# Tile 0 transposed before its scale is known: a linear-attention and MLP kernel with its start reordered

## The chip, the cores and the metric

The kernel runs on one core of one Trainium2 chip. The metric is the device time of one execution, in microseconds (us); lower is better. A core has TensorE (PE in the profile; PEld is its loading of weights), VectorE (DVE), ScalarE (ACT), GpSimd (POOL) and SyncE (SP). SP here only issues DMAs. Each engine works through its own instructions in order.

## The reference

`x` has 2048 tokens of 512 features. The block normalises each token, and adds to `x` the output of a linear attention with 32 heads and that of an MLP with a squared ReLU, both reading the same normalised tokens. All is in float32.

```python
x = A_x
xn = _layernorm(x)                      # (x - mean) / sqrt(var + 1e-5)
# attention: 32 heads of 16
q, k, v = split(xn @ wqkv)
phi = lambda t: where(t > 0, t + 1, exp(t)) + 1e-6
kv  = einsum("bhsd,bhse->bhde", phi(k), v);   z = sum over s of phi(k)
num = einsum("bhqd,bhde->bhqe", phi(q), kv);  den = phi(q) . z + 1e-6
att = (num / den) @ wo
# MLP, F = 1376
h   = relu(xn @ w1 + b1) ** 2
mlp = h @ w2 + b2
out = x + att + mlp
```

## The kernel before, in words

The 2048 tokens are 16 tiles of 128 tokens; four tiles make a block of 512. A float32 operand is split into a high part (rounded to the type fp32r) and a low part (what is left), and a product is three matmuls: high by high, high by low and low by high. "Chunk j" is one of the four groups of 128 features. Order on every engine is the order in which the program was recorded (`manual_schedule`).

**First phase, tiles 0 to 15 (L594 to L903).** For each tile i: statistics on VectorE (`measure`), 1/deviation as a power on GpSimd (`roots`), the normalised tile `xp[i]`, its transposed columns, and the split of the columns into `xsb` (`high` on ScalarE, `low` on VectorE). `project` multiplies the columns with the key weights `wk` (split into `wkh` by `heads_k` on ScalarE and `wkl` by `rests_k`) into a PSUM bank `pk`. `phi_k` makes phi of the keys, `parts` splits it, `tokens` splits the token-major `xp[i]` into `tok[i]`, and `kx(i)` accumulates, over all tiles, the product of tokens and keys. The last feature of `xp[i]` is overwritten with ones first (`ones(i)`, on GpSimd), so that the same product also holds the sum of the keys; the values are worked out from the accumulated product later. Weights and tokens are loaded on SP's queue.

**How tiles are transposed.** Tiles 0 to 2 (`i < NDVE`, which is 3) go through TensorE, against an identity, 128 by 128 at a time (`turned_pe`). The others go through DRAM: the normalised tile is written to `via`, read back in four moves that put blocks of 32 rows where they belong (`regroup`, `move`), and VectorE's transposition of 32 by 32 blocks ends it (`turn`). Such a tile is written into `xp` in a grouped order (`gjc`), and `tokens` and `ones` look at `i >= NDVE` to know it. `ones(i)` of such a tile has to come after `via` was written, since it overwrites a feature.

The columns of tiles 0 to 7 are kept in DRAM (`xTd`) for the second half of the kernel, which reads them back around 197 us (`keep_t` writes them; for tiles 0 to 2 ScalarE first copies them out of PSUM).

**The start, L525 to L669.** `WARM` matmuls of zeros run first. Tiles 0 and 1 and the four chunks of the key weights `rk` are loaded on SP's queue; ScalarE's queue holds one small load named `touch`, ahead of its table load. Tiles 0 to 2 share the three `pk` banks, and the products of tile 0 and tile 1 are interleaved by hand, chunk by chunk (`some`, `rest`). `load_x(4, x4)` fetches tiles 4 to 7, one megabyte, in one DMA; a one-column copy on GpSimd from `xp[1]` into `x4` just ahead of it makes the load wait until tile 1 is normalised.

**Later phases** (L905 on): the MLP and queries of two blocks at a time in a seven-product scheme, the attention's output and the sums. The change doesn't touch them.

## Time and profile before

| what | value |
|---|---|
| time, median of 3 runs | 408.75 us (408.64 to 409.38) |
| profiled execution, its own time | 409.03 us |
| its span | 407.3 us |
| PE busy | 402.2 us of the span |
| DVE, ACT, POOL busy | 308.0, 268.4, 49.7 us |
| granted TensorE clock in the windows shown | 1.00 |
| first transpose on TensorE | at 6.14 us |
| kx(0) | from 16.35 us |

How to read the lines of the profile. A timeline row is: start in us from the span's start, how long the merged instructions took, engine, line of the kernel, operation, output<-inputs by the program's names, shapes, how many; in brackets the idle time of that engine before it and what ended it. `SPq` is SP's DMA queue; its rows give the time of the issue, not of the transfer. A row of the DMA view ends with the size and the median us from issue to landing. A row of the stretches ("0.00:8.00 8.00, ...") gives the length, then busy time and count of PE, PEld, DVE, ACT and POOL, the granted clock, the busy share of the DMA engines and GB/s. A row of the chain is start, length, engine and line. A row of one line's instructions gives shortest/median/longest duration in ns.

### The profile page before, as it was taken

The numbers are of one execution on the slowest core, as the hardware profiler recorded it, in microseconds if no ns is written. First come the engines' busy times: TensorE is split into PE (matmuls) and PEld (weight loads), VectorE is DVE, ScalarE is ACT, GpSimd is POOL, SyncE is SP. The second block draws the span as 40 slices with busy tenths as digits, with TensorE's granted clock in tenths as the row PEclk, the third lists the DMA queues.
The fourth block names the chain that finished last, engine by engine and source line by source line (L and its number), as shares of the span: only waits on it lengthen the run. The fifth ranks groups of instructions, "written<-read, shape, count | busy, mean of one in ns | idle before, by whom it ended". The sixth has DMA issues, their size and how long they took to land.

```text
span 407.3 us, 5632 instructions
## 1 busy us (share of the span) xinstructions
PE 402.2 (99%) x1939; PEld 331.0 (81%) x1939; DVE 308.0 (76%) x559; ACT 268.4 (66%) x466; POOL 49.7 (12%) x81
## 2 busy tenths in 40 slices
PE   8999999999999999999999999999999999999996
PEld 7888888888788888888878888888888888878885
DVE  5886666587898989988349997667989676449833
ACT  5677677556887788886818752667687856828520
POOL 5444333220000000030000300000000200001200
PEclk9999999999999999999999999999999999999999
DMA  6857646900432231380564903311222880034612
GB/s 212 278 175 224 208 163 192 256 27 0 120 90 80 77 103 27 121 200 16 217 228 146 194 19 113 106 53 52 52 80 50 226 189 26 0 108 151 105 26 103
DMA packets 46830, 49.00 MB, mean 120 GB/s; under 512 B 8337, under 2 KB 31121, under 8 KB 46546
## 3 DMA queue, kind: packets, MB, share of 16 engines
q1 hardware_dynamic: 44418, 44.46, 35.4%
q0 software_dynamic: 2304, 4.20, 6.5%
q8 instruction: 15, 0.25, 0.2%
q14 instruction: 13, 0.11, 0.1%
q10 hardware_dynamic: 80, 0.00, 0.0%
HBM read 37.76 MB, written 9.70 MB: 117 GB/s over the span
## 4 chain that ended last, share of the span: by engine, by line
PE 98%; DMA 1%; DVE 1%; ACT 0%; issue 0%
PE acc L133 37%; PE b L497 33%; PE pk L378 11%; PE kx L398 11%; PE acc L508 2%; PE pz L133 1%; DMA x<-in_A_x_dram 1%; PE b L133 1%; PE pz0b L133 1%; PE acc L515 0%; PE pt L310 0%; DVE st L236 0%; PE pkv L937 0%; PE pm L954 0%; PE end L133 0%; PE end L508 0%
## 5 line engine op out<-in xcount | busy, mean ns | idle before, releaser
L133 PE MATMUL acc<-w2r,s 128*128 128x512 f32 x477 | 112.8, 390 | 0.0
L133 PEld LDWEIGHTS acc<-w2r,s 128*128 128x128 f32 x477 | 89.4, 188 | 19.3 <-issue 0.7
L497 PE MATMUL b<-T,aop 128*128 128x512 f32 x336 | 83.5, 389 | 0.0
L497 PEld LDWEIGHTS b<-T,aop 128*128 128x128 f32 x336 | 63.0, 188 | 13.9 <-ACT t L114 0.8
L1075 POOL DMA_DIRECT2D res<-in_B_b_dram x16 | 14.4, 1067 | 276.7 <-DVE pt L438 90.4
L398 PE MATMUL kx<-pk,tok 128*128 128x512 f32 x192 | 46.0, 389 | 0.0
L398 PEld LDWEIGHTS kx<-pk,tok 128*128 128x128 f32 x192 | 36.0, 188 | 7.6 <-ACT pk L114 0.2
L497 PE MATMUL b<-xs0h,aop 128*128 128x512 f32 x112 | 36.9, 390 | 0.0
L133 PE MATMUL acc<-mh,aTsr 128*128 128x512 f32 x112 | 35.6, 389 | 0.0
L1083 DVE TENSOR_TENSOR res<-acc,res 128x512 f32<-128x512 f32 x16 | 10.7, 689 | 20.5 <-PE acc L133 19.2
L114 ACT ACTIVATE aop<-S 128x512 fp32r<-128x512 f32 x28 | 17.5, 624 | 12.5 <-DVE S L735 12.5
L359 POOL TENSOR_TENSOR tok<-xp,tok 128x512 fp32r<-128x512 f32 x15 | 20.2, 1344 | 39.6 <-ACT tok L114 39.6
L497 PEld LDWEIGHTS b<-xs0h,aop 128*128 128x128 f32 x112 | 21.0, 188 | 4.4
L133 PEld LDWEIGHTS acc<-mh,aTsr 128*128 128x128 f32 x112 | 21.0, 188 | 4.4
L125 DVE TENSOR_TENSOR w2r<-r,w2r 128x512 fp32r<-128x512 f32 (+2 forms) x35 | 23.8, 682 | 0.5 <-ACT w2r L114 0.4
L122 DVE TENSOR_TENSOR aop<-S,aop 128x512 fp32r<-128x512 f32 x28 | 19.3, 688 | 4.8 <-ACT aop L114 4.4
L122 DVE TENSOR_TENSOR s<-c,s 128x512 fp32r<-128x512 f32 x20 | 13.6, 689 | 11.4 <-ACT s L114 11.3
L497 PE MATMUL b<-xs0l,aop 128*128 128x512 f32 x56 | 21.8, 389 | 0.0
L133 PE MATMUL acc<-ml,aTsr 128*128 128x512 f32 x56 | 21.8, 389 | 0.0
L114 ACT ACTIVATE w2r<-r 128x512 fp32r<-128x512 f32 x32 | 19.6, 619 | 3.3 <-DMA out_dram<-res 2.0
L497 PE MATMUL b<-xs1h,aop 128*128 128x512 f32 x56 | 19.5, 389 | 0.0
L114 ACT ACTIVATE T<-Tf 128x512 fp32r<-128x512 f32 x16 | 9.5, 624 | 14.4 <-DVE Tf L678 14.3
(195 smaller groups left out, 751.6 us busy)
## 6 DMA issues: line engine op xcount, KB each, us to landing
r<-in_B_w_dram SPq DMA_DIRECT2D x49, 256.0 KB, 3.2
res<-in_A_x_dram SPq DMA_DIRECT2D x8, 512.0 KB, 4.2
res<-in_B_b_dram POOLq DMA_DIRECT2D x16, 256.0 KB, 5.7
out_dram<-res SPq DMA_DIRECT2D x15, 256.0 KB, 2.1
via<-xp SPq DMA_DIRECT2D x5, 512.0 KB, 2.6
xg<-via SPq DMA_DIRECT2D x20, 128.0 KB, 2.8
xTd<-t SPq DMA_DIRECT2D x8, 256.0 KB, 3.4
x<-in_A_x_dram SPq DMA_DIRECT2D x4, 512.0 KB, 4.1
```

Source lines behind the costliest of these rows:

```text
L114: nc.scalar.activation(o, i, AF.Copy, bias=bias)
L122: ENG[el].tensor_tensor(out=l, in0=src, in1=f32(h), op=OP.subtract)
L125: nc.vector.tensor_tensor(out=l, in0=src, in1=f32(h), op=OP.subtract)
L133: nc.tensor.matmul(ps, lhsT=a[u], rhs=b[v], start=first and n == 0, stop=last and n == 2)
L359: ENG[el].tensor_tensor(out=l, in0=src, in1=f32(h), op=OP.subtract)
L378: nc.tensor.matmul(ps, lhsT=cols(i)[u][:, j, slot(i)], rhs=w[v][:, j, :], start=first and n == 0, stop=last and n == len(steps) - 1)
L398: nc.tensor.matmul(kxp[c], lhsT=tok[i][:, u, c * P:(c + 1) * P], rhs=pk[i][:, v], start=i == 0 and (u, v) == first, stop=i == NT - 1 and ( ...
L497: nc.tensor.matmul(ps, lhsT=a[u][:, j * P:(j + 1) * P], rhs=b[v][:, j, :], start=first and j == 0 and n == 0, stop=last and j == 1 and n == 2,
L508: nc.tensor.matmul(ps, lhsT=s[u][:, k * P:(k + 1) * P], rhs=w2s[NF - 1][u][:, a:z], start=first and u == 0, stop=stop and u == 1)
L1075: nc.gpsimd.dma_start(r[:, i], b2[None, :].partition_broadcast(P), accum_op=OP.add)
L1083: nc.vector.tensor_tensor(out=r[:, a:z], in0=ps, in1=r[:, a:z], op=OP.add)
```

## The change

Tile 0 is centred as soon as its mean is known and transposed like that; 1/deviation is a factor of each token, so it is put in where the tokens stand on partitions. The keys of tile 0 come out of the projection unscaled, and phi of them is worked out with the scale (`scale0`, and its negative `less0`, which GpSimd makes). The normalised tile, still needed for `tok[0]`, is made later by a ScalarE activation with that scale, written in the grouped order into the place of the raw tile `x0`, so tile 0 joins the set `grouped`. Its normalised columns, which `keep0` used to store from PSUM, come through `via0`: written after `keep1`, read back by four moves at tile 9, turned by VectorE and stored at tile 10. Tile 0 is loaded in two halves of 256 features on SP's queue, tile 1 on ScalarE's queue; `touch` is gone; `WARM` is 9 instead of 11. Tiles 0 and 1 share one `group`, so one power serves both. The hand-written order of the first products changes, and `rests_k("dve", 1)` comes earlier.

The diff, cut where a line only moves:

```diff
-    WARM = 11
+    WARM = 9
...
-    touch = keep.tile([D // Q * 4, 1], F32, name="touch")
-    nc.scalar.dma_start(touch, wqkv.rearrange("(a b) c -> a b c", b=Q // 4)[:, 0, D:D + 1])
     nc.scalar.preload_act_table_set("natural_log_exp_and_others")
...
+    grouped = {*range(NDVE, NT)}
...
-    def load_x(i, t):
+    def load_x(i, t, eng=nc.sync):
...
@@ turned_pe
-        ones(i)
+        if i:
+            ones(i)
...
@@ ones
-        nc.gpsimd.memset(xp[i][:, D - 1:] if i < NDVE else xp[i][:, NJ - 1, P - 1:], 1.0)
+        nc.gpsimd.memset(xp[i][:, NJ - 1, P - 1:] if i in grouped else xp[i][:, D - 1:], 1.0)
...
@@ the loads
-    for i in range(2):
-        load_x(i, t[:, i:i + 1])
+    xr[0] = t[:, 0]
+    left, right = slice(0, D // 2), slice(D // 2, D)
+    for a in (left, right):
+        nc.sync.dma_start(xr[0][:, a], xf[:P, a])
+    load_x(1, t[:, 1:], nc.scalar)
...
@@ the start
-    two_tiles = group(0), group(1)
-    for t in two_tiles:
-        measure(t)
-        roots(*t)
-    for k in range(2):
-        a = slice(k * D // 2, (k + 1) * D // 2)
-        nc.vector.tensor_scalar(xp[0][:, a], xr[0][:, a], two_tiles[0][2][:, 0, 0:1], two_tiles[0][3][:, 0, :1],
-                                op0=OP.subtract, op1=OP.mult)
-    high, low, keep0 = transposed(0, 2)
+    two_tiles = group(0, 1)
+    _, st, mv, y = two_tiles
+    for k, a in enumerate((left, right)):
+        nc.vector.bn_stats(st[:, k, :], xr[0][:, a])
+    nc.vector.bn_aggr(mv[:, 0, :], st[:, :2, :])
+    for a in (left, right):
+        nc.vector.tensor_scalar(xp[0][:, a], xr[0][:, a], mv[:, 0, 0:1], None, op0=OP.subtract)
+    high, low, _ = transposed(0, 2)
+    high()
+    high(1)
     heads_k(0)
-    high()
+    measure(two_tiles, 1)
+    roots(*two_tiles)
+    low()
+    some(0, 0, (0,), True)
+    some(0, 1, (0,))
     rests_k("pool", 0)
-    some(0, 0, (0,), True)
-    normalise(*two_tiles[1])
+    nc.vector.tensor_scalar(xp[1], xr[1], mv[:, 1, 0:1], y[:, 0, 1:2], op0=OP.subtract, op1=OP.mult)
+    low(1)
+    heads_k(1)
+    some(0, 0, (1,))
+    some(0, 1, (1,))
     high1, low1, keep1 = transposed(1, 2)
-    heads_k(1)
+    scale0 = y[:, 0, 0:1]
+    less0 = y[:, 1, 0:1]
+    nc.gpsimd.tensor_scalar(less0, scale0, -1.0, None, op0=OP.mult)
     nc.gpsimd.tensor_copy(x4[:, 0, :1], xp[1][:, :1])
     load_x(4, x4)
...
@@ after the products of tiles 0 and 1
-    keep0()
     keep1()
+    xp0 = xr[0].rearrange("p (g n) -> p g n", g=NJ)
+    nc.scalar.activation(xp0.rearrange("p g (j c) -> p g j c", j=NJ), gjc(xp[0]), AF.Copy, scale=scale0)
+    xp[0] = xp0
+    grouped.add(0)
+    via0 = dram.tile([P, NJ, P], F32, name="via0")
+    nc.sync.dma_start(via0, xp0)
+    ones(0)
...
-    phi_k(0, pks[0])
+    kp[0] = w512("k0", "p", 6)
+    kept = w512("k0r", "p", 6)
+    nc.scalar.activation(kp[0], pks[0], AF.Relu, scale=less0)
+    nc.vector.tensor_scalar(kept, pks[0], scale0, 0.0, op0=OP.mult, op1=OP.max)
+    nc.scalar.activation(kp[0], kp[0], AF.Exp, scale=-1.0)
+    nc.vector.tensor_tensor(out=kp[0], in0=kept, in1=kp[0], op=OP.add)
...
@@ tile 9
             load_o()
+            xg0 = w512("xg0", "raw", 6).rearrange("p (g n) -> p g n", g=NJ)
+            of_0 = via0.rearrange("(r t) g n -> g t r n", r=NJ)
+            for g in range(NJ):
+                nc.sync.dma_start(xg0[32 * g:32 * (g + 1)], of_0[g])
...
@@ tile 10
+            t0 = w512("t0", "p", 6).rearrange("p (j t) -> p j t", j=NJ)
+            turn(t0, xg0)
+            nc.sync.dma_start(xTd[0][:, :, slot(0)], t0)
```

Three places in the order of the instructions, before and then after. The semaphores in brackets are what an instruction waits for; DMAHW3 and the like are those of DMAs.

VectorE from its first instruction, before: `st0`, `mv0`, `y0` are tile 0's statistics, mean and variance, and root; `st1` and so on tile 1's; `x0` holds both raw tiles.

```order
L236 BN_STATS st0_143<-x0_112 128x6 [waits DMAHW1_49]
L237 BN_AGGR mv0_144<-st0_143 128x2 [waits DVE_49]
L247 TENSOR_SCALAR y0_145<-mv0_144 128x1 [waits DVE_49]
L236 BN_STATS st1_146<-x0_112 128x6 [waits DMAHW2_49]
L237 BN_AGGR mv1_147<-st1_146 128x2 [waits DVE_49]
L247 TENSOR_SCALAR y1_148<-mv1_147 128x1 [waits DVE_49]
L600 TENSOR_SCALAR xp0_80<-x0_112,mv0_144,y0_145 128x256 [waits Pool_49]
L600 TENSOR_SCALAR xp0_80<-x0_112,mv0_144,y0_145 128x256
L270 TENSOR_SCALAR xp0_80<-x0_112,mv1_147,y1_148 128x512 [waits Pool_49]
```

VectorE after, from its first instruction:

```order
L600 BN_STATS st0_140<-x0_108 128x6 [waits DMAHW0_49]
L600 BN_STATS st0_140<-x0_108 128x6 [waits DMAHW1_49]
L601 BN_AGGR mv0_141<-st0_140 128x2 [waits DVE_49]
L603 TENSOR_SCALAR xp0_78<-x0_108,mv0_141 128x256 [waits DVE_49]
L603 TENSOR_SCALAR xp0_78<-x0_108,mv0_141 128x256
L235 BN_STATS st0_140<-x0_108 128x6 [waits DMAHW3_49]
L236 BN_AGGR mv0_141<-st0_140 128x2 [waits DVE_49]
L246 TENSOR_SCALAR y0_142<-mv0_141 128x2 [waits DVE_49]
L329 TENSOR_TENSOR xs1l_75<-pt00_148,xs1h_74 128x2x128 [waits Activation_49]
L614 TENSOR_SCALAR xp0_78<-x0_108,mv0_141,y0_142 128x512 [waits Pool_49]
```

Tile 0's subtraction no longer waits for GpSimd, and tile 1's statistics stand behind it.

GpSimd from the first power to the low part of tile 0's tokens, before (`y2` and `y3` belong to tiles 2 and 3; the L348 rows are the memsets of ones, of tiles 0, 1 and 2 in this order):

```order
L248 TENSOR_TENSOR y0_145<-y0_145,power_99 128x1 [waits DVE_49,Pool_49]
L248 TENSOR_TENSOR y1_148<-y1_148,power_99 128x1 [waits DVE_49]
L348 MEMSET xp0_80 128x1 [waits DVE_49,PE_49]
L583 TENSOR_TENSOR wkl_73<-rk_113,wkh_72 128x512 [waits DMAHW3_49,Activation_49]
L348 MEMSET xp0_80 128x1 [waits DVE_49,PE_49]
L611 COPY x4_134<-xp0_80 128x1
L247 TENSOR_SCALAR y2_197<-mv2_196 128x1 [waits DVE_49]
L248 TENSOR_TENSOR y2_197<-y2_197,power_99 128x1 [waits Pool_49]
L247 TENSOR_SCALAR y3_209<-mv3_208 128x1 [waits DVE_49]
L248 TENSOR_TENSOR y3_209<-y3_209,power_99 128x1 [waits Pool_49]
L348 MEMSET xp0_80 128x1 [waits DVE_49,PE_49]
L359 TENSOR_TENSOR tok0_279<-xp0_80,tok0_279 128x512 [waits Activation_49]
```

GpSimd after, over the same stretch (the L348 rows are now those of tiles 1, 0 and 2):

```order
L247 TENSOR_TENSOR y0_142<-y0_142,power_97 128x2 [waits DVE_49,Pool_49]
L586 TENSOR_TENSOR wkl_71<-rk_109,wkh_70 128x512 [waits DMAHW2_49,Activation_49]
L348 MEMSET xp0_78 128x1 [waits DVE_49,PE_49]
L622 TENSOR_SCALAR y0_142<-y0_142 128x1 [waits Pool_49]
L624 COPY x4_131<-xp0_78 128x1
L246 TENSOR_SCALAR y2_191<-mv2_190 128x1 [waits DVE_49]
L247 TENSOR_TENSOR y2_191<-y2_191,power_97 128x1 [waits Pool_49]
L246 TENSOR_SCALAR y3_202<-mv3_201 128x1 [waits DVE_49]
L247 TENSOR_TENSOR y3_202<-y3_202,power_97 128x1 [waits Pool_49]
L348 MEMSET x0_108 128x1 [waits DMAHW3_49,DMAHW1_49,Activation_49]
L348 MEMSET xp0_78 128x1 [waits DVE_49,PE_49]
L359 TENSOR_TENSOR tok0_274<-x0_108,tok0_274 128x4x4x32 [waits DMAHW0_49,Activation_49]
```

Tile 0's memset moved from the third place to the tenth and waits for DMAs, the one on DMAHW3 being the write of `via0`. The negation L622 stands ahead of the pacing copy L624.

SP's queue from the load of tiles 4 to 7, before:

```order
L161 DMA x4_134<-in_A_x_dram 128x4x512 [waits DMAHW1_49,Pool_49]
L338 DMA xTd0_93<-t0_226 512x1x128 [waits DMAHW2_49,Activation_49]
L338 DMA xTd0_93<-t1_230 512x1x128 [waits DMAHW3_49,Activation_49]
L283 DMA via3_236<-xp0_80 128x512 [waits DMAHW4_49,DVE_49]
L161 DMA x8_135<-in_A_x_dram 128x2x512 [waits DMAHW5_49]
```

SP's queue after, from the same load:

```order
L160 DMA x4_131<-in_A_x_dram 128x4x512 [waits DMAHW1_49,Pool_49]
L338 DMA xTd0_91<-t1_219 512x1x128 [waits DMAHW2_49,Activation_49]
L658 DMA via0_224<-x0_108 128x512 [waits DMAHW3_49,Activation_49]
L282 DMA via3_229<-xp0_78 128x512 [waits DMAHW4_49,DVE_49]
L160 DMA x8_132<-in_A_x_dram 128x2x512 [waits DMAHW5_49]
```

Tile 0's transposed store gave its place to the write of `via0`, which is third behind the megabyte. On ScalarE the copy of tile 0's tokens stands ahead of that of its keys in both kernels.

More of the change, by code (lines that the diff above doesn't have):

```diff
@@ L627 @@
     heads_k(2)
-    rests_k("dve", 1)
     high1(1)
```

13 lines of the change are left out of this document (5 added, 8 removed).

## Prediction

> **What bounds the kernel now.** I read the page's engine shares first, then the chain that ended last. All times are microseconds from the span's start unless they are called durations.
>
> ```profile
> PE 402.2 (99%) x1939; PEld 331.0 (81%) x1939; DVE 308.0 (76%) x559; ACT 268.4 (66%) x466; POOL 49.7 (12%) x81
> PE 98%; DMA 1%; DVE 1%; ACT 0%; issue 0%
> 0.00:8.00 8.00, 6.28 (x32) 5.69 (x33) 3.70 (x11) 3.28 (x6) 4.46 (x17) 1.00 0.75 256
> 8.00:16.00 8.00, 8.00 (x38) 6.30 (x38) 7.17 (x15) 5.50 (x13) 3.66 (x9) 1.00 0.83 246
> 24.00:407.00 383.00, 379.92 (x1837) 312.48 (x1835) 289.79 (x520) 253.76 (x438) 38.44 (x51) 1.00 0.40 114
> ```
>
> TensorE is the chain, and from 8.0 it hardly rests. The change removes no product. It can move the end in two ways only: by starting the unbroken stream of products sooner, or by tearing a hole into it. The chain in order of time shows where the stream begins and where the accumulation kx, the first reader of tile 0's keys and tokens, starts:
>
> ```profile
> 0.79 2.85 DMA x<-in_A_x_dram
> 7.99 4.38 PE pk L378 x19
> 16.51 5.47 PE kx L398 x24
> ```
>
> **The start.** Timeline rows of the load, VectorE, TensorE and ScalarE, and the landings of the loads from the DMA view (issue, then duration to landing):
>
> ```profile
> 1.25 0.41 SPq L161 DMA_DIRECT2D x<-in_A_x_dram  x1
> x<-in_A_x_dram SPq DMA_DIRECT2D x1, 256.0 KB, 3.1
> rk<-in_A_wqkv_dram SPq DMA_DIRECT2D x1, 256.0 KB, 4.3
> 3.66 0.69 DVE L236 BATCH_NORM_STATS2 st<-x 128x6 f32<-128x512 f32 x1 [3.66 <-DMA x<-in_A_x_dram]
> 4.39 0.18 DVE L237 BATCH_NORM_AGGREGATE mv<-st 128x2 f32<-128x6 f32 x1
> 5.68 0.73 DVE L600 TENSOR_SCALAR xp<-x,mv,y 128x256 f32<-128x256 f32 x2
> 6.54 0.55 DVE L270 TENSOR_SCALAR xp<-x,mv,y 128x512 f32<-128x512 f32 x1
> 6.14 0.76 PE L310 MATMUL pt<-ident,xp 128*128 128x128 f32 x4 [0.74 <-DVE xp L600]
> 8.53 0.39 PE L378 MATMUL pk<-wkl,xs1h 128*128 128x512 f32 x1
> 6.62 0.39 ACT L326 ACTIVATE xs1h<-pt 128x256 fp32r<-128x256 f32 x1 [0.75 <-PE pt L310]
> 6.90 0.62 ACT L114 ACTIVATE wkh<-rk 128x512 fp32r<-128x512 f32 x1
> ```
>
> Removed in front of the first transpose: GpSimd's power and tile 1's statistics, which today lie between the load's landing at 3.65 and L600 at 5.68. Added: a second statistics instruction. Neither a 256-wide statistics instruction nor a load of half a tile is in the trace. I take 0.42 for the first, since the 256-wide subtraction takes 0.41 (two of them span 0.73, stepped by 0.32) and the 512-wide statistics 0.69; at 0.69 it would cost 0.27 more. The right half lands at about 3.65, when the whole tile lands now, if tile 1's load on ScalarE's queue stays out of its way. It lands at 1.25 + 3.1 = 4.35, as tile 1 does now, if those 256 KB go ahead of it. So the first centred half is ready at 3.65 + 0.42 + 0.05 + 0.18 + 0.05 + 0.41 = 4.75, or at 5.45. The first transposes start at 4.8 to 5.5 instead of 6.14, a gain of 0.65 to 1.35.
>
> The Trainium skill (DMA: Bandwidth & Descriptors, "Queues, rings and completion order") says that a DMA engine alternates between the queues that have work, a packet at a time. By it tile 1 is served between the two halves, and the sum below would end at its upper figure; with the two loads in order of issue it would end at its lower one. No row of before has two large loads on two queues.
>
> That gain doesn't survive to the third product. ScalarE copies both halves of tile 0 and then the weights. The first copy starts 0.48 after the transposes (6.62 − 6.14), so at 5.3 to 6.0; two copies and wkh of chunk 0 (0.39 and 0.62, overlapping by about 0.1) end at 6.5 to 7.2. The weights of chunk 1 landed at 6.5 (the row of rk, issued at 2.18), and no edit moves them; wkh of chunk 1 is done at 7.1 to 7.8. TensorE's new order puts four products ahead of tile 1's transposes, and the last two of them read chunk 1: 7.15 + 2 × 0.23 + 8 passes × 0.11 puts the end of those transposes (call it T) at 8.5. At the late end of the range tile 1's own path decides: its statistics, one power for both tiles and the subtraction give 8.2, so T = 9.1. Today the product that follows them, L378 with wkl, starts at 8.53. So the first transposes come 0.65 to 1.35 sooner and the stream is 0.0 to 0.6 later.
>
> **The new wait.** Tile 0's tokens now pass through DRAM like tile 3's. The memset of ones into tile 0 must wait until that write (via0) has landed; ScalarE's copy of tile 0's tokens waits for the memset, and behind that copy, on ScalarE in order, stands the copy of tile 0's keys, without which kx(0) can't start. Before, the memset came at 6.97. So the question is when via0 lands. On SP's queue it stands behind the megabyte x4 and one transposed store:
>
> ```profile
> 8.55 0.38 SPq L161 DMA_DIRECT2D x<-in_A_x_dram  x1
> x<-in_A_x_dram SPq DMA_DIRECT2D x1, 1024.0 KB, 5.2
> 10.08 0.62 SPq L338 DMA_DIRECT2D xTd<-t  x1
> xTd<-t SPq DMA_DIRECT2D x1, 256.0 KB, 4.4
> 13.43 0.34 SPq L283 DMA_DIRECT2D via<-xp  x1
> via<-xp SPq DMA_DIRECT2D x1, 256.0 KB, 2.4
> 6.97 0.16 POOL L348 MEMSET xp<- 128x1 f32 x1 [0.46 <-PE pt L310]
> 8.34 0.19 POOL L611 COPY x<-xp 128x1 f32<-128x1 f32 x1
> 9.68 0.58 POOL L247 TENSOR_SCALAR y<-mv 128x1 f32<-128x1 f32 x1 [1.16 <-DVE mv L237]
> 14.70 0.62 ACT L114 ACTIVATE tok<-xp 128x512 fp32r<-128x512 f32 x1
> 15.56 0.64 ACT L114 ACTIVATE pk<-k 128x512 fp32r<-128x512 f32 x1 [0.24 <-DVE k L373]
> 16.35 5.63 PE L398 MATMUL kx<-pk,tok 128*128 128x512 f32 x24
> ```
>
> These transfers land in the order of their issue: x4 at 8.55 + 5.2 = 13.75, the first store at 10.08 + 4.4 = 14.5, tile 3's write at 13.43 + 2.4 = 15.85. Between the last two lies the other store, so each takes some 0.7.
>
> - x4 is issued behind GpSimd's pacing copy. The copy now waits for tile 1's transposes (T), a memset of 0.1 and the new negation on one column, which by L247's row costs 0.58; with its own 0.19 that is T + 0.97, so 9.5 to 10.1 instead of 8.55.
> - x4 lands 5.2 later, at 14.7 to 15.3. Worked out from 256 KB at 2.8 and three more at 0.7, it would be 4.9, so this is sure to 0.3.
> - The store of tile 1 and via0 follow at 0.7 each: via0 lands at 16.1 to 16.7. ScalarE's rescaling of tile 0, which feeds it, comes after tile 1's copies, near 11, and is well covered by this queue.
> - Memset and semaphores 0.2; then from the start of the token copy to kx, 16.35 − 14.70 = 1.65 today, of which 0.24 was ScalarE's wait for the keys. That leaves 1.4, so kx(0) starts at 17.7 to 18.3.
>
> Against 16.35 that is 1.35 to 1.95 of TensorE standing still. I take the middle, 1.6, since nothing in the rows decides between the two places of tile 1's load.
>
> **Edits that I cost at nothing.** Tile 0's phi becomes four instructions; the extra multiplication on VectorE (0.69, as L373) runs beside the exponential (0.63), and the whole phi would be done near 15.6, ahead of the late token copy. Two copies of tile 0's columns (0.39 each) leave ScalarE and one rescaling (0.6 to 0.8) comes. If this cover went, each would cost under 0.2. After kx(0), GpSimd's low part of the tokens (1.3) ends some 2.2 after via0's landing, ahead of the products that read it by about 0.2. Two warm-up matmuls fewer cost nothing if the clock is granted as early as now (a rival, below). At tile 9 SP issues four more moves behind wo, and VectorE one more turn:
>
> ```profile
> 64.80 0.41 SPq L197 DMA_DIRECT2D wo<-in_A_wo_dram  x1
> 67.44 0.35 SPq L283 DMA_DIRECT2D via<-xp  x1
> 59.33 1.75 SPq L291 DMA_DIRECT2D xg<-via  x4
> 74.44 0.71 DVE L295 STREAM_TRANSPOSE xT<-xg 128x512 f32<-128x512 f32 x1 [2.79 <-DMA xg<-via]
> ```
>
> SP is free from 65.2 to 67.4, and four moves take 1.75. The turn takes 0.7 on an engine that idles 2.79 soon after. Without that cover VectorE would be 0.7 late there, with TensorE's next need of its columns several microseconds away.
>
> **Rivals.**
>
> *The write is early (no change).* If the DMA engines served via0 without regard to the megabyte ahead, it would land about 2.4 after an issue near 11.3, so at 13.7; the point from which it costs nothing is a landing by 14.6. Then the stream goes through, 0.0 to 0.6 later than now: 409.0 to 409.6 in the profile's terms, 408.75 to 409.35 in the median's. Against it stand the landings in order of issue. Chance 0.15.
>
> *The clock is granted late (slower still).* Of the warm-up passes some run at 0.42 and the last at 0.27:
>
> ```profile
> L528 PE MATMUL warm<-const-float32-0.0 x22: 273/421/552, 0.8 to 5.1; 128*128 128x128 f32 x22
> 0.83 3.96 PE L528 MATMUL warm<-const-float32-0.0 128*128 128x128 f32 x17 [0.83 <-PEq L1389]
> ```
>
> Seventeen passes are slow in this run; eighteen are left after the change. If the change of speed came after them, tile 0's and tile 1's transposes (12 passes, 0.11 more each) and four products (0.23 more each) would run at half rate ahead of T. Behind chunk 1's weights lie eight of the passes (0.9 more) and two of the products (0.45 more); with the switch somewhere within them I take 1.0 for T and so for the end: 411.35 in the median's terms. Chance 0.07.
>
> The Trainium skill (TensorE: Matmul & The Clock Gate, Part 1) says that the full clock follows a busy window of about 3.4 us whose phase is free-running, so that the warm-up's length in time counts. Its rule agrees with the slow-then-fast passes here, and it would let that phase differ from run to run.
>
> *The lead holds (faster).* If chunk 1's weights and tile 1 came sooner than I reckon and via0 were early too, up to the 1.35 of the first transposes would reach the end: 407.4. It needs both; the landing of rk at 6.5 speaks against it. Chance 0.07.
>
> **The numbers.** The profiled run took 409.03 (span 407.3 and 1.7 around it); the median of the runs is 408.75, so I take off 0.28. Forecast: 409.03 + 1.6 − 0.28 = 410.35. Its own ends are 410.1 and 410.7; with the unknown prices on each side (0.3 for x4, 0.27 for the statistics) 409.8 to 411.0. The forecast has 0.71. Ten per cent left out on each side gives 409.1 to 411.2: into the unchanged case below, into the late clock above. About 0.2% (0.8 us) is what a measurement of this kernel can tell. Slower by more: forecast 0.71 and late clock 0.07, so 0.78; within it: 0.15; faster: 0.07.
>
> **What would show it.** Right: the first transposes at 4.8 to 5.5; T at 8.5 to 9.1; x4's issue about one microsecond later than 8.55; GpSimd idle before the memset of tile 0 until a DMA named via; the token copy of ScalarE near 16.4 to 17.0 with a wait for GpSimd; a hole of over a microsecond on TensorE before kx(0), and none after. Wrong: kx(0) at 16.5 or earlier, via0 landed before 14.6, or a hole elsewhere, at tile 3's columns or at tile 10's turn.

## The result, and the profile after

| | before | after |
|---|---|---|
| median | 409.14 us (6 runs, 408.64 to 409.38) | 412.32 us (6 runs, 412.09 to 412.83) |
| profiled execution, its span | 409.03, 407.3 | 412.09, 410.4 |
| end of tile 1's transposes (T) | 7.99 | 10.14 |
| first product of keys and tokens, kx(0) | 16.35 | 19.05 |

The ratio is 1.0081, interval 1.0068 to 1.0094: slower, by 3.2, where 1.6 was forecast. The range ended at 411.2. All times are microseconds from the span's start unless they are called durations.

The chain in order of time, after (start, length, what). In before it reaches TensorE's unbroken stream of products at 7.99; here it runs over other engines and DMAs until 19.05:

```profile
1.24 2.96 DMA x<-in_A_x_dram
...
5.54 0.61 DVE st L235
...
6.72 0.72 POOL y L247
7.45 0.03 issue
7.47 1.51 DVE xp L614
8.98 0.04 issue
9.02 0.70 PE pt L309 x2
...
12.03 0.72 ACT x L654
...
12.87 4.71 DMA via<-x
...
17.84 0.63 ACT tok L113
18.48 0.53 ACT pk L113
19.00 0.04 issue
19.05 5.80 PE kx L398 x24
```

The store via0 is on it, as forecast. But ahead of it stand tile 1's power and tile 1's subtraction L614 (its line shifts by one or two in other runs), which alone takes 1.51 where the same subtraction of before took 0.55. TensorE's timeline shows how little of the 2.70 by which kx(0) is late is the hole, TensorE's idle time just before it:

```profile
5.42 0.63 PE L309 MATMUL pt<-ident,xp 128*128 128x128 f32 x4 [0.75 <-DVE xp L603]
7.10 0.50 PE L378 MATMUL pk<-wkh,xs1h 128*128 128x512 f32 x1 [1.05 <-ACT wkh L113]
9.02 1.11 PE L309 MATMUL pt<-ident,xp 128*128 128x128 f32 x4 [0.18 <-DVE xp L614]
9.79 0.78 PE L378 MATMUL pk<-wkl,xs1h 128*128 128x512 f32 x1
14.12 0.60 PE L309 MATMUL pt<-ident,xp 128*128 128x128 f32 x4
19.05 0.73 PE L398 MATMUL kx<-pk,tok 128*128 128x512 f32 x2 [0.62 <-ACT pk L113]
```

The hole is 0.62. Tile 2's transposes stand at 14.12, against 12.21 before: the stream is already 1.91 late there. Its passes beside tile 1's transposes are slow (0.78 for a product of 0.39), and the stretches say why (length, busy time and count of PE, PEld, DVE, ACT, POOL, granted clock, DMA, GB/s):

```profile
0.76:4.17 3.41, 3.34 (x16) 3.37 (x17) 0.43 (x1) 1.28 (x1) 2.00 (x9) 1.00 0.65 217
4.17:7.58 3.41, 1.61 (x10) 1.02 (x9) 2.64 (x9) 1.70 (x4) 0.86 (x2) 1.00 1.01 344
7.58:10.99 3.41, 3.23 (x11) 2.24 (x10) 3.14 (x5) 1.24 (x4) 1.59 (x4) 0.50 0.14 55
11.00:14.41 3.41, 3.41 (x17) 2.77 (x17) 3.34 (x9) 1.72 (x4) 2.13 (x4) 1.00 0.60 227
```

The clock was granted at 4.17, taken back at 7.58 and granted again at 11.0. (Its records begin with the first grant; ahead of it the column shows 1.00, though the passes are slow.) In the stretch before it was taken back TensorE was busy for 1.61 of 3.41. The same stretch before, with TensorE busy for 2.52 of 3.41:

```profile
4.77:8.18 3.41, 2.52 (x17) 1.86 (x16) 2.84 (x8) 2.18 (x6) 2.45 (x4) 1.00 0.96 351
```

The sum of after, against before: T 2.15 later; from T to kx(0) 8.91 instead of 8.36, so 0.55; from kx(0) to the end 391.34 instead of 390.95, so 0.39. Together 3.09, the difference of the spans (410.39 and 407.30). T isn't quite the same place in both: before has one product ahead of tile 1's transposes, and after has four, at 0.23 each. So some 0.7 of T's 2.15 are products that moved ahead of it. The product that follows four others in both, the first with wkl, starts at 9.79 instead of 8.53, 1.26 later.

### The profile page after: what moved, and what is told of

Same layout as the page of the kernel before. It is cut to its first block, busy times and chain, and to the rows that moved or that the text cites. A ratio compares the mean times of both kernels' runs of the same rounds, so it can differ in the third digit from the quotient of the medians.

```text
span 410.4 us, 5642 instructions
## 1 busy us (share of the span) xinstructions
PE 403.4 (98%) x1935; PEld 331.2 (81%) x1935; DVE 310.4 (76%) x561; ACT 269.0 (66%) x465; POOL 48.8 (12%) x81
## 3 DMA queue, kind: packets, MB, share of 16 engines
HBM read 38.02 MB, written 9.96 MB: 117 GB/s over the span
## 4 chain that ended last, share of the span: by engine, by line
PE 95%; DMA 2%; DVE 1%; ACT 1%; issue 0%; POOL 0%; SPq 0%; POOLq 0%
PE acc L132 37%; PE b L497 33%; PE kx L398 11%; PE pk L378 9%; PE acc L508 2%; PE pz L132 1%; DMA via<-x 1%; DMA x<-in_A_x_dram 1%; PE b L132 1%; PE pz0b L132 1%; DVE xp L614 0%; PE acc L515 0%; PE pkv L964 0%; DVE st L235 0%; PE pm L981 0%
## 5 line engine op out<-in xcount | busy, mean ns | idle before, releaser
L359 POOL TENSOR_TENSOR tok<-xp,tok 128x512 fp32r<-128x512 f32 x14 | 18.5, 1324 | 38.8 <-ACT tok L113 38.8
```

The costliest lines, as they stand in the source:

```text
L359: ENG[el].tensor_tensor(out=l, in0=src, in1=f32(h), op=OP.subtract)
```

## The experiments

My theory at the start: the loss is made by the start (clock, L614) and by the store. The rivals: the store alone, as forecast; or the tiles from 9 on. Each kernel was timed in five rounds beside before on the same chip; before took 409.1 to 409.2 in each set. The intervals reach half a microsecond and more to each side, so that where two kernels differ by less, the times alone don't tell them apart and the profiles have to. "Without the columns' route" means the kernel whose tile 0 columns lack the factor 1/deviation.

### The first four: the start in pieces

**e1_clock.** More warming products, and four more to fill the rest ahead of the first product.

```diff
-    WARM = 9
+    WARM = 13
...
+    for _ in range(4):
+        nc.tensor.matmul(pw[:, :P], lhsT=zeros, rhs=zeros, start=True, stop=True)
     some(0, 0, (0,), True)
```

> The changed kernel with 13 warm-up matmuls and four more matmuls of zeros between tile 0's transposes and its first product, so that TensorE doesn't rest there. Theory A (the second half-rate stretch of the clock, from 7.6 to 11.0, comes from TensorE's two rests at 4.7 and 6.05, and costs time in the stream of products): the clock stays full after 4.2, tile 1's transposes end near 9.7 instead of 10.1, the product after them has no slow steps, x4 is issued near 10.4, kx(0) starts near 18.6; 411.8 to 411.9 against 412.3, with a larger hole before kx(0) (about 1.4). Theory B (the landing of via0 alone decides): the same 0.4, and nothing from the faster stream. Theory C (the clock is no matter, its second stretch has another cause): the half-rate stretch stays, 412.3.

Measured 412.2, ratio 1.0077 [1.0064, 1.0089]: nothing won. The edit spoilt its own question: at half clock 13 products last until 6.7 and push tile 0's transposes from 5.42 to 6.51, and with them ScalarE's copies and the first product, which came at 8.27. (The first weights landed late too, at about 6.6, but ScalarE, in order, came to them only at 7.58.) T is 9.96. In its profile the clock wasn't taken back. Tile 1's subtraction takes 0.54 there, since GpSimd's work on the weights starts behind it.

**e2_wkl0_vector.** The low part of the weights' first chunk (`rests_k`) by VectorE, behind L614, instead of by GpSimd.

```diff
-    rests_k("pool", 0)
     nc.vector.tensor_scalar(xp[1], xr[1], mv[:, 1, 0:1], y[:, 0, 1:2], op0=OP.subtract, op1=OP.mult)
     low(1)
+    rests_k("dve", 0)
```

> The changed kernel with the low part of the first weight chunk on VectorE, behind tile 1's subtraction, instead of on GpSimd beside it. Theory A (VectorE's subtraction of tile 1 took 1.50 instead of 0.55 because GpSimd's wkl ran at the same time): L614's instruction takes 0.55, tile 1 is ready near 8.0, its transposes then follow the products at 8.65 at half rate and end near 9.7; x4 near 10.3; kx(0) near 18.6; 411.9. Rival (it waits or runs long for another reason, its inputs or semaphores): the subtraction still takes 1.5 and the time stays at 412.3 or rises, since VectorE has 0.68 more to do.

411.81, 1.0071 [1.0054, 1.0089]. VectorE's and GpSimd's timelines of after, then VectorE's of e2:

```profile
7.47 1.50 DVE L614 TENSOR_SCALAR xp<-x,mv,y 128x512 f32<-128x512 f32 x1 [0.58 <-POOL y L247]
7.42 1.27 POOL L586 TENSOR_TENSOR wkl<-rk,wkh 128x512 fp32r<-128x512 f32 x1
```

```profile
7.49 0.55 DVE L613 TENSOR_SCALAR xp<-x,mv,y 128x512 f32<-128x512 f32 x1 [0.57 <-POOL y L247]
```

The same subtraction, started at the same time, takes 0.55 as soon as GpSimd isn't working beside it. That part is shown.

**e3_early_x4.** GpSimd's pacing copy and the load of tiles 4 to 7 right behind tile 1's subtraction.

```diff
+    nc.gpsimd.tensor_copy(x4[:, 0, :1], xp[1][:, :1])
+    load_x(4, x4)
     low(1)
...
-    nc.gpsimd.tensor_copy(x4[:, 0, :1], xp[1][:, :1])
-    load_x(4, x4)
```

> The changed kernel with the pacing copy and the load of tiles 4 to 7 recorded right behind tile 1's subtraction, ahead of the memset that waits for tile 1's transposes and of the negation. x4 is then issued near 9.2 instead of 10.8 and via0 lands near 16.0. Theory A (two causes: a stream that is 1.9 late, and a hole of 0.8 behind via0): the hole goes, kx(0) starts at 18.3, 411.5. Theory B (via0's landing alone decides): kx(0) starts 1.6 earlier, 410.7. If the landing doesn't follow x4's issue, nothing moves.

411.47, 1.0058 [1.0046, 1.007]. The load is issued at 9.44 instead of 10.80, the store lands at 16.27 instead of 17.57 and the hole is down to 0.08. kx(0) is at 18.06. (The clock was kept in this profile, and T is 9.88, so 0.26 of the 0.99 at kx(0) were won ahead of the store.) So the landing of the megabyte sets the hole, and a stream that is late by 1.7 stands behind it.

**e4_three.** The three edits together.

> All three edits together: a full clock, wkl of chunk 0 on VectorE, x4 issued early. Theory A: tile 1's transposes end near 8.6, the stream is about where the kernel before has it, x4 is issued near 8.4, via0 lands near 15.2, kx(0) starts at 16.4 to 16.7; 409.2 to 409.8, that is within 0.2% of the kernel before. If something else than these three holds the start back, 410.5 or more is left.

411.31, 1.0054 [1.0041, 1.0067]: the three don't add up, and the expectation is missed by 1.5. T is 9.31, kx(0) 17.85 behind a new hole of 0.42.

### The next four: before with one edit, and the store

**e5_before_warm9.** The kernel before, `WARM = 9`.

> The kernel before with 9 instead of 11 warming products and nothing else. Theory 'clock withdrawn' (TensorE's rests inside the 3.41 us behind the grant send the clock back to half for another 3.41 us): the two products fewer move the grant forward to about 4.2, the rest of 4.7 to 6.1 lies in the window behind it, and the clock falls back once: 409.9 to 410.7. Rival 'the clock costs nothing here' (TensorE is held by loads and other engines until 8 us whatever its clock): 409.0 to 409.5.

410.54, 1.0034 [1.0021, 1.0046]. Two warming products fewer cost the kernel before 1.46. In this profile the clock isn't taken back: it comes late. The stretches up to the grant at 9.97:

```profile
3.15:6.56 3.41, 2.25 (x11) 1.92 (x11) 2.61 (x8) 0.63 (x1) 1.25 (x3) 1.00 0.96 321
6.56:9.97 3.41, 3.36 (x12) 2.58 (x11) 2.37 (x5) 2.56 (x7) 1.60 (x4) 1.00 0.53 201
```

That the clock is half ahead of the grant, where its column has no record yet, is seen from TensorE's timeline, where four transposes take 1.11 and 1.05 at 6.17 and 7.92, as at half clock after, instead of 0.76 and about 0.6:

```profile
6.17 1.11 PE L310 MATMUL pt<-ident,xp 128*128 128x128 f32 x4 [1.16 <-DVE xp L600]
7.92 1.05 PE L310 MATMUL pt<-ident,xp 128*128 128x128 f32 x4
17.84 2.50 PE L398 MATMUL kx<-pk,tok 128*128 128x512 f32 x10
```

T is 8.97 (7.99 before), kx(0) 17.84 (16.35). In three of the other four runs of e5 the mean clock is 0.996, as in after, where it was taken back for 3.41; the time is the same.

**e6_no_columns.** No store, moves or late turn; the columns kept from the transposes (`keep0`) as before.

```diff
-    via0 = dram.tile([P, NJ, P], F32, name="via0")
-    nc.sync.dma_start(via0, xp0)
...
-            for g in range(NJ):
-                nc.sync.dma_start(xg0[32 * g:32 * (g + 1)], of_0[g])
...
-        if i == 10:
-            turn(t0, xg0)
```

> The changed kernel without the store, the moves and the late turn of tile 0's columns: the columns are kept from the transposes as before, so tile 0's columns lack the factor 1/deviation. Theory 'two pieces, start and store' (the stream is 1.9 late by its start, the wait of tile 0's tokens for the store adds 0.8, the edits at tiles 9 and 10 add nothing): the hole before the first keys-by-tokens product closes to 0.0 to 0.2, that product at 18.2 to 18.5, 411.3 to 411.7. Rival 'the late edits cost too' (the moves on SyncE's queue push the store of tiles 12 and 13 from 67.4 to 70.9): a further 0.3 to 0.5 off, 410.9 to 411.3. Rival 'the hole is handed on' (ScalarE's copies of the columns, two of about 0.3, delay the tokens as much): 412.0 to 412.4.

410.81, 1.0048 [1.0031, 1.0064]: 1.5 off. The hole is 0.07, kx(0) at 17.81, with T still at 9.64. So the columns' route costs about half of the loss, and the other half is there without it. It is there although L614 takes only 0.55 in this profile: the weights landed at about 7.1, and GpSimd, which works on them, started at 7.86, behind L614's start at 7.48.

**e7_via_act.** `nc.scalar.dma_start(via0, xp0)`.

> The changed kernel with tile 0's store issued on ScalarE's queue instead of SyncE's, and nothing else. Theory 'place in the queue' (the store lies behind the megabyte of tiles 4 to 7 on SyncE's queue, so that it lands 17.57, 1.8 behind it): it lands at 14.8 to 15.9, the ones of tile 0 are set by 16.1, the hole closes to 0.0 to 0.2, 411.3 to 411.7. Rival 'the transfers share the engines anyway': lands at 16.8 to 17.5, the hole stays over 0.5, 412.0 to 412.5.

412.49, 1.0081 [1.0068, 1.0094]. The store, issued at 12.89 on ScalarE's queue, still lands 4.8 later:

```profile
x<-in_A_x_dram SPq DMA_DIRECT2D x1, 1024.0 KB, 5.2
xTd<-t SPq DMA_DIRECT2D x1, 256.0 KB, 5.6
via<-x ACTq DMA_DIRECT2D x1, 256.0 KB, 4.8
```

The megabyte issued at 10.92 lands at 16.1, tile 1's store at 17.9 and via0 at 17.7. Tile 1's store landed at 16.6 in after, so the two stores now seem to share what the megabyte leaves. My theory of the queue's place falls; what e3 moved was the megabyte itself. The hole is 0.10 in this profile, where over 0.5 was expected, and still kx(0) is at 19.26: the clock was slow from 9.13 to 12.54 here, so the stream is late by as much as the store.

**e8_wkh_first.** ScalarE rounds the weights' first chunk ahead of both halves of tile 0's columns.

```diff
+    heads_k(0)
     high()
     high(1)
-    heads_k(0)
```

> The changed kernel with ScalarE rounding the first chunk of weights ahead of both halves of tile 0's columns, where it rounded them behind. Theory 'the rest of 1.05 before the first product is ScalarE's order' : first product at 6.7 to 6.9 instead of 7.10, TensorE's rest 0.6 to 0.8; with the clock still withdrawn 411.9 to 412.2, with the clock kept 411.2 to 411.6. Rival 'the weights' landing': where the first chunk lands at 5.7 or later, as in two of five profiles, the first product comes at 7.4 or later and nothing is won, 412.2 to 412.6.

412.3, 1.0087 [1.0073, 1.01]. The first product comes at 6.91 and TensorE's idle time ahead of it shrinks from 1.05 to 0.77. What is won is lost at the next step:

```profile
6.91 0.50 PE L378 MATMUL pk<-wkh,xs1h 128*128 128x512 f32 x1 [0.77 <-ACT xs1h L326]
...
9.10 0.65 PE L309 MATMUL pt<-ident,xp 128*128 128x128 f32 x4 [0.66 <-DVE xp L614]
```

### The clock put right, and the route again

**e9_warm11.** After with `WARM = 11`.

> The changed kernel with 11 warming products, as before, instead of 9, and nothing else. In ten profiles the clock is granted behind a stretch of 3.41 us in which TensorE was busy for 0.85 of it or more, and taken back behind one in which it was busy for 0.52 or less; kept at 0.55 and more. Theory 'two products fewer open the rest' : with 11 the rest ahead of the transposes goes (0.75 to 0.0 to 0.2), the stretch behind the grant holds only the rest of about 1.0 before the first product and stays over 0.55, the clock is kept in nearly all runs (mean clock 0.998 to 1.0); tile 1's transposes end at 9.1 to 9.6, the first keys-by-tokens product at 17.9 to 18.5: 410.8 to 411.6. Rival 'not the clock': as with 13 and a filling (412.2): 412.0 to 412.5.

412.13, 1.0068 [1.0055, 1.0081]: 0.2 under after. The clock was kept (mean 0.999 and more in all five runs, against 0.995 to 0.998 in after's six), and T moved only from 10.14 to 9.75, since tile 1's transposes wait 0.67 for L614. My theory was right on the clock and wrong on its price: in after the slow clock lies mostly beside a wait that is there anyway. At kx(0) it is worth 0.40 (18.65 against 19.05). A new hole of 0.21 stands before kx at 87.38.

**e10_warm11_no_columns.** e9 without the columns' route.

> 11 warming products, and tile 0's columns kept from the transposes as before (they lack the factor 1/deviation): no store, no moves, no late turn. Theory 'warming products and the columns' route are the loss' (1.4 as measured in the kernel before, 1.5 as measured without the columns): 409.0 to 409.7. Rival 'they overlap' (either one opens the same hole): 410.4 to 410.9, as without the columns alone.

410.67, 1.0045 [1.0033, 1.0057]: the rival is right. The clock is kept, no store is waited for, the hole is 0.07, and kx(0) still starts at 17.84. All of this is T, which is 9.66.

**e11_with_touch.** e10 with the early read of wqkv (`touch`) back.

> As the kernel with 11 warming products and without the columns' route, and with the early read of one number of each 32 rows of wqkv, which the change had left out, back on ScalarE's queue. The first chunk of the weights landed between 4.90 and 7.13 in eight profiles without that read, and at 5.21 and 5.71 in two with it. Theory 'the early read spares the late packets': the chunk lands by 5.8, 0.2 to 0.5 under the same kernel without it: 408.8 to 409.4. Rival 'chance': within 0.2 of it, and a landing over 6 can come here too.

411.08, 1.0047 [1.0034, 1.0061], against 410.67 without it. The runs go from 410.34 to 412.45, too wide for the 0.2 to 0.5 that was asked; in the profile, the slowest of them, the first product comes at 7.51 (7.08 without). The first chunk of the weights was expected by 5.8; it landed at about 6.1, and at 5.8 in e10, without `touch`. Nothing speaks for `touch` as a cause, and less than half a microsecond of it stays open.

**e12_own_tile.** Whole change, `WARM = 11`, `touch`, and a second copy of the scaled tokens for the store.

```diff
+    xv0 = w512("xv0", "raw", 6).rearrange("p (g n) -> p g n", g=NJ)
+    nc.scalar.activation(xv0.rearrange("p g (j c) -> p g j c", j=NJ), gjc(xr_0), AF.Copy, scale=scale0)
-    nc.sync.dma_start(via0, xp0)
+    nc.sync.dma_start(via0, xv0)
```

> The changed kernel with 11 warming products and the early read of wqkv, and with a second copy of tile 0's scaled tokens, made by ScalarE right behind the first (0.71), from which the store is made, so that the ones of tile 0 wait for no store. Theory 'the wait for the store is the hole': tokens of tile 0 at 15.0 to 16.0, the hole closes to 0.0 to 0.2, the first keys-by-tokens product at 16.9 to 17.4, and the late edits cost 0.0 to 0.4: 409.5 to 410.3. Rival 'the late edits are the cost of the columns': the hole closes but the tiles from 9 on lose 1.0 or more: 410.5 to 411.2.

411.38, 1.0055 [1.0043, 1.0067]. The hole is 0.07 and the ones of tile 0 are set at 14.13, so the wait for the store is the hole. T is 10.09 and kx(0) 18.31, so the expected 409.5 to 410.3 was missed by the start, not by the store.

### What sets T

The base of the next three is e10 (410.67, T 9.66, kx(0) 17.84).

**e13_wkl0_vector.** The edit of e2 on e10.

> The kernel with 11 warming products and without the columns' route (tile 0's columns lack the factor 1/deviation), with the rest of the first chunk of weights made by VectorE behind tile 1's subtraction instead of by GpSimd beside it. That base takes 410.67, its subtraction 1.50, tile 1's transposes end at 9.66, the first keys-by-tokens product starts at 17.84. Theory 'the end of tile 1's transposes sets it all': the subtraction takes 0.55, the transposes end at 8.7 to 9.0, the product at 16.9 to 17.2, 409.7 to 410.1. Rival 'the products in front of the transposes hold them' (five products stand ahead on TensorE): transposes end at 9.3 or later, 410.3 to 410.7.

410.33, 1.0031 [1.0019, 1.0043]. L613 takes 0.55. T gains 0.76 (8.90), kx(0) 0.55 (17.29), the median 0.34; the expected 409.7 to 410.1 is missed by 0.2.

**e14_stats_first.** Tile 1's statistics between tile 0's halves, both deviations ahead of tile 0's subtractions.

```diff
+    nc.vector.bn_stats(st[:, 0, :], xr[0][:, left])
+    nc.vector.bn_stats(st[:, 2, :], xr[1])
+    nc.vector.bn_aggr(mv[:, 1, :], st[:, 2, :])
+    nc.vector.bn_stats(st[:, 1, :], xr[0][:, right])
     nc.vector.bn_aggr(mv[:, 0, :], st[:, :2, :])
+    roots(*two_tiles)
```

> The same base with tile 1's statistics on VectorE between the two halves of tile 0, and both tiles' deviation ahead of tile 0's subtractions, so that GpSimd's power starts at about 5.6 instead of 6.72. Theory 'VectorE's order': tile 0's transposes come 0.6 to 0.8 later, tile 1's subtraction starts at 6.4 to 6.6, ahead of GpSimd's work on the weights, and takes 0.55 to 0.8; tile 1's transposes end at 8.0 to 8.6, the product at 16.3 to 16.9, 409.1 to 409.7. Rival 'what is won at tile 1 is lost at tile 0': 410.3 to 410.8.

410.54, 1.0041 [1.0029, 1.0053]: the rival, within 0.13 of the base. In its profile, the slowest of its five runs, L615 starts at 7.34 and takes 0.54, but tile 0's transposes begin at 6.14, as in before, and the clock is taken back.

**e15_x1_on_sync.** `load_x(1, t[:, 1:])`, on SyncE's queue.

> The same base with tile 1's tokens on SyncE's queue behind the two halves, as before, instead of on ScalarE's. Theory 'tile 1 takes tile 0's place at the engines': the halves land at 2.9 to 3.2 and 3.4 to 3.6 instead of 3.6 and 4.2, tile 1 at 4.2 to 4.5; tile 0's transposes and all behind come 0.5 to 0.7 earlier: 409.9 to 410.2. Rival 'the weights then land later by what the queue is longer' (one issue, 0.47): the first product no earlier than before, 410.5 to 410.9.

410.28, 1.0031 [1.0019, 1.0043], 0.39 off. VectorE's timeline of after and of e15:

```profile
3.66 0.98 DVE L600 BATCH_NORM_STATS2 st<-x 128x6 f32<-128x256 f32 x2 [3.66 <-DMA x<-in_A_x_dram]
4.92 0.62 DVE L603 TENSOR_SCALAR xp<-x,mv 128x256 f32<-128x256 f32 x2
```

```profile
2.94 0.94 DVE L600 BATCH_NORM_STATS2 st<-x 128x6 f32<-128x256 f32 x2 [2.94 <-DMA x<-in_A_x_dram]
4.16 0.62 DVE L603 TENSOR_SCALAR xp<-x,mv 128x256 f32<-128x256 f32 x2
```

Tile 1's load on its own queue takes 0.72 from tile 0's left half, on the chain of after. But here TensorE doesn't take it up. With 11 warming products it is still at these when the half is ready, and the transposes begin behind them, with no idle time:

```profile
0.83 5.03 PE L528 MATMUL warm<-const-float32-0.0 128*128 128x128 f32 x22 [0.83 <-PEq L1407]
5.66 0.74 PE L309 MATMUL pt<-ident,xp 128*128 128x128 f32 x4
```

So the first product didn't come sooner (7.44 against 7.08). The gain at T, 0.53, comes from L614: it starts at 6.97, ahead of GpSimd's work on the weights (7.47), and takes 0.54.

**e16_first_own.** Whole change with `WARM = 11`, e14's order and e12's second copy.

> The whole change (columns' route included, nothing left out) with 11 warming products, tile 1's statistics first on VectorE as in the kernel named stats first, and a second copy of tile 0's scaled tokens for the store, so that no ones wait for it. Theory 'three causes, start, order, store': the product at 16.6 to 17.2, the late edits cost 0.0 to 0.5: 409.4 to 410.2, so no gain over before even then. Rival 'the lead is real once freed': 408.4 to 408.9. Rival 'the late edits': 410.3 to 411.0.

411.11, 1.0054 [1.0039, 1.0069]: 0.57 over e14, which lacks the route. kx(0) was 17.61 in the profile.

**e17_whole.** Whole change, `WARM = 11`, with the edits of e8, e12 (without `touch`) and e15.

> The whole change, nothing left out, with 11 warming products, tile 1's tokens on SyncE's queue behind the halves, the first chunk of weights rounded by ScalarE ahead of tile 0's columns, and a second copy of tile 0's scaled tokens for the store. Theory 'the end of tile 1's transposes sets the run': the first product at 6.6 to 6.9, the transposes end at 8.3 to 8.7, the first keys-by-tokens product at 16.5 to 17.0, the end 391.3 behind: 409.5 to 410.1. Rival 'a lead is there': transposes end under 8.0, 408.4 to 409.0. Rival 'the weights land late' (the first chunk at 5.4 to 6.0): the first product at 7.2 and later, 410.2 to 411.0.

410.78, 1.0037 [1.0025, 1.0049]. The first product came at 6.56, as expected, and L614 is long again, since with the weights rounded sooner GpSimd starts sooner too. VectorE and GpSimd of e17:

```profile
6.88 1.39 DVE L614 TENSOR_SCALAR xp<-x,mv,y 128x512 f32<-128x512 f32 x1
6.71 1.28 POOL L586 TENSOR_TENSOR wkl<-rk,wkh 128x512 fp32r<-128x512 f32 x1
```

T is 8.98, kx(0) 17.14.

**e18_whole_no_columns.** The same without the columns' route.

> The same without the second copy, the store, the moves and the late turn: the columns are kept from the transposes as before and lack the factor 1/deviation. Theory: the same start, the end 391.0 behind the first keys-by-tokens product: 0.2 to 0.5 under the kernel with the columns' route, 409.2 to 409.7. Rival 'a lead is there': 408.2 to 408.7. Rival 'the columns' route costs nothing once no ones wait for the store': within 0.15 of the other.

410.37, 1.0029 [1.0018, 1.004]: 0.41 under e17 (0.2 to 0.5 expected), T 9.04. None of the 18 beats before; e15, e13 and e18 come nearest, 1.2 above it. T under 8.0 was not reached. e17 with e2's edit, the one combination that the rows still call for, was not run.

## Why the prediction was wrong, by its own steps

**The sign and the store's chain: right.** First transposes at 5.42 (4.8 to 5.5 forecast). The later of the two landings came: tile 1, issued at 0.82, landed 3.0 later, ahead of tile 0's right half at 4.20. The Trainium skill (DMA: Bandwidth & Descriptors, "Queues, rings and completion order") has the queues served in turn, and e15 agrees: without the second queue the left half is there 0.72 sooner. From T on each link held: the megabyte's issue T + 0.66 (0.97 forecast, the negation took 0.25 and not 0.58), landing 5.0 later (5.2), via0 1.8 behind it (1.4), kx(0) 1.5 behind that (1.6). From T to kx(0) it is 8.91; the forecast's 17.7 less 8.5 is 9.2. GpSimd's idle before the memset is as told:

```profile
17.71 0.10 POOL L348 MEMSET x<- 128x1 f32 x1 [3.69 <-DMA via<-x]
```

**The step that failed: T.** Forecast 8.5, or 9.1 where tile 1's own path decides; measured 10.14. That path did decide. Against its sum, which had L614 end at 8.2 and T at 9.1:

- L614 was to end at 8.2; at before's 0.55 that is a start at 7.65. It started at 7.47, 0.18 sooner, and took 1.50, 0.95 more. The two rows stood side by side in the new order and I gave each its price alone. Before, GpSimd's work on the weights started at 7.06, when the subtraction (6.54 to 7.09) was all but done; after, GpSimd's power releases both, and GpSimd starts first, by 0.05. e2 and e13 show it by taking GpSimd away; e14, e15 and e16, where L614 starts first, have it at 0.54. The Trainium skill (GPSIMD Engine Reference, "8. Key points") says that GpSimd shares its way into SBUF with VectorE and names the forms of VectorE's instructions that contend; I cited no price for it. The measured one is 0.95, and 0.84 in e17.
- From L614's end to T I had 0.9; it was 1.16, at half clock. At full clock e10 needs 0.71 (8.95 to 9.66).

Sum: 9.1 − 0.18 + 0.95 + 0.26 = 10.13. The working with "8 passes" was wrong besides, since four stand in tile 1's row (and eight, not 12, in those of both tiles); worked with four, the other path gives 8.1. That is too early as well: with L614 short, this path decides, and the runs put it at 8.90 (e13) and, at half clock, 9.60 (e2). So taking L614's 0.95 away gave 0.76 and 0.54 at T.

**The clock.** The rival "granted late" had 0.07 and 1.0. Its edit, alone in the kernel before, costs 1.46 (e5). I asked only whether the grant comes in time, and missed that it is taken back. In after it mattered little (0.40 at kx(0), 0.2 in the median, e9), because L614 was the later wait; with L614 short, T is 9.60 at half clock (e2) and 8.90 at full clock (e13).

**The hole.** I put 1.35 to 1.95 of the loss there and 0.0 to 0.6 on the stream; measured 0.62 and 1.91. A late stream hides the wait behind it: the store is issued by the same chain, and T moves both.

**Edits costed at nothing.** The columns' route costs more than its wait. With the wait gone it is 0.41 (e18 to e17) and 0.57 (e14 to e16), both no wider than the intervals; with the wait 1.46 (e10 to e9). Two parts can be read. From the last tile's kx to the end it is 312.19 to 312.26 in the eleven profiles with the route, and 312.01 to 312.08 in the nine without it, before among them. That is 0.15 to 0.2 in every run; from TensorE's last product to the end it is 3.54 in after and 3.38 in before, so it lies there, in rows that don't name its cause. The other part lies between kx of tile 12 and that of tile 15 (0.48 from e10's profile to e9's, of 1.62 in all, of which 0.81 are there at kx(0)) and goes back, as the rows suggest, to SP's queue at tile 9. SP's queue of before, e10 and e9 there:

```profile
67.44 0.35 SPq L283 DMA_DIRECT2D via<-xp  x1
```

```profile
69.19 0.35 SPq L282 DMA_DIRECT2D via<-xp  x1
```

```profile
68.61 1.97 SPq L848 DMA_DIRECT2D xg<-via  x4
70.68 0.38 SPq L282 DMA_DIRECT2D via<-xp  x1
```

The write of the next tiles stands behind tile 0's moves, 1.5 later than in e10, of which 0.8 is e9's later kx(0). VectorE waits for the value weights, which are loaded behind it on the same queue, for 4.08 in e9 (2.59 in e10, 1.22 in before), and then TensorE, in e9, has a hole:

```profile
84.67 0.69 DVE L719 TENSOR_TENSOR wv<-wv,wvl 128x512 f32<-128x512 f32 x1 [4.08 <-DMA wvl<-in_A_wqkv_dram]
```

```profile
87.38 1.85 PE L398 MATMUL kx<-pk,tok 128*128 128x512 f32 x7 [0.21 <-ACT pk L113]
```

I had looked at the turn, which costs nothing, and at SP's free time, and not at what is loaded behind the moves. e1 and e8 have the same hole (0.45 and 0.19). In after's profile this wait is 3.72 and no hole opens, so it decides in some starts only. From kx of tile 12 to that of tile 15, six of the eleven profiles with the route lose 0.2 to 0.7 against before, and none of the nine without loses anything. That the moves alone make it was not tested apart from the store.

**What stays open.** In all 20 profiles kx(0) stands 8.1 to 9.0 behind T, and with no wait for the store and the clock kept 8.15 to 8.4, so T sets it. With the clock kept and L614 short, T is still 8.90 to 9.64 (e13, e15, e16 and e6). There it stands 1.69 to 1.81 behind the first product, so the four products ahead of tile 1's transposes decide. And the first product came at 7.08 or later wherever ScalarE rounds the weights behind tile 0's columns, against 7.05 before: the lead of tile 0's transposes was gone there. e8, e17 and e18 round the weights first and have it at 6.91, 6.56 and 6.62; L614 is long in all three. The lead also has a floor in the warming products. In e11, e12, e15, e17 and e18, all with 11 of them, the transposes begin right behind them, at 5.51 to 5.66, and 9 instead of 11 cost the kernel before 1.46.

Each wait taken away uncovered the next, and I don't know that they can all be taken away at once. With e2's edit on e17, T would be 6.56 + 1.69 = 8.25 and kx(0) some 16.4 to 16.6, near before's 16.35; that is an estimate from e17, e13 and the distances above, not a run. Also open is why e13's gain at T comes to the end only in part: between kx(0) and kx of tile 6 its stream loses 0.66 against before, where e10's loses 0.18.

## What to carry to other kernels

A step that starts earlier is worth what the last of its partners allows: follow the second tile's path as closely as the first's, and price two instructions by the rows in which they run together, not each by itself. Ask also which of the two starts first. When an edit shortens a warm-up or opens rests near the start, ask whether the clock is kept as well as when it comes. When a transfer is added to a queue, look at what is loaded behind it, not only at whether the queue is free.

## What the runs showed of the hardware

**The clock changed in steps of 3.41, and was taken back behind stretches that were half busy.** In 20 profiles the stretches of 3.41 that lead to the grant had TensorE busy for 0.83 or more; stretches of 0.77 (e12), 0.73 (e1) and 0.66 (e5) led to none. After the grant it was taken back behind stretches of 0.44 (e14), 0.47 (after), 0.48 (e11), 0.49 (e2) and 0.52 (e7), and kept behind 0.54 (e9), 0.55 (e3) and all above. The two that stand nearest each other, e7 and e9:

```profile
5.72:9.13 3.41, 1.78 (x8) 0.88 (x7) 2.76 (x6) 1.70 (x4) 1.96 (x2) 1.00 0.78 293
9.13:12.54 3.41, 3.40 (x10) 2.86 (x11) 3.08 (x8) 2.64 (x7) 1.30 (x5) 0.50 0.05 19
```

```profile
3.66:7.07 3.41, 1.84 (x15) 1.44 (x13) 2.96 (x9) 1.13 (x4) 0.28 (x1) 1.00 1.02 335
7.07:10.48 3.41, 2.62 (x11) 1.60 (x12) 2.92 (x5) 1.47 (x5) 2.17 (x5) 1.00 0.35 134
```

The first grant came between 3.66 and 6.86, and in e5 at 9.97, one stretch later; so the phase differs from run to run. The Trainium skill (TensorE: Matmul & The Clock Gate, Part 1) gives the window's length, which agrees, and has the clock fall back after an idle window; here a window that was half busy was enough.

**VectorE and GpSimd together: who starts first.** In the ten profiles in which GpSimd's subtraction of 128x512 starts ahead of VectorE's of the same size (by 0.05 to 0.19), VectorE's takes 1.39 to 1.51 and ends 0.28 or 0.29 behind GpSimd's, which keeps its 1.26 to 1.29. In the other ten VectorE starts first, or GpSimd has no such work, and it takes 0.54 or 0.55. In e6 the two overlap with VectorE ahead, and VectorE isn't slowed:

```profile
7.48 0.55 DVE L614 TENSOR_SCALAR xp<-x,mv,y 128x512 f32<-128x512 f32 x1 [0.51 <-POOL y L247]
7.86 1.32 POOL L586 TENSOR_TENSOR wkl<-rk,wkh 128x512 fp32r<-128x512 f32 x1 [0.41 <-ACT wkh L113]
```

What VectorE has next can pay instead: its own part of the weights takes 1.27 to 1.37 beside GpSimd's in e1, e6, e14, e15 and e16, and 0.68 alone.

**A DMA issue didn't wait for the table load.** It was issued at 0.82, beside a load that ran from 0.79 to 2.07. ScalarE's timeline of after:

```profile
0.79 1.28 ACT L77 ACT_TABLE_LOAD   x1 [0.79 <-PEq L1416]
0.82 0.39 ACTq L160 DMA_DIRECT2D x<-in_A_x_dram  x1
```
